# Output weights of six head pairs in 2, 4 or 8 loads of fewer partitions instead of one load of 128

## The chip, the cores and the metric

The kernel runs on one core of a Trainium2 chip. The metric is the device time of one execution in microseconds (us). A core has a matrix engine (TensorE, PE in the profile; its weight loads are PEld), VectorE (DVE), ScalarE (ACT), GpSimd (POOL), and SyncE (SP), which here does nothing but wait on semaphores and issue transfers. Transfers are carried out by 16 DMA engines. On-chip memory (SBUF) has 128 partitions; a tile's first dimension is its partitions.

## The reference

One token goes through a gated mix of two blocks: `out = g*a + (1-g)*b`, with `g = sigmoid(sum(x * gate_w))`. Block b is a layernorm of `x` (448 numbers), a small MLP over 1792 hidden units with a tanh-gelu, and a sum; it needs little data. Block a is attention for one query token with 16 query heads and 8 key/value heads over a cache of 65536 positions of 256 numbers, bf16:

```python
q = (x @ wq)                                  # 448 -> 16 heads x 256
k = jnp.repeat(k_cache, 2, axis=1)            # k_cache, v_cache: [1, 8, 65536, 256]
v = jnp.repeat(v_cache, 2, axis=1)
scores = jnp.einsum("bhqd,bhkd->bhqk", q, k) * (Dh ** -0.5)
p = softmax(scores, axis=-1)
o = jnp.einsum("bhqk,bhkd->bhqd", p, v)
a = o.transpose(0, 2, 1, 3).reshape(B, Sq, Hq * Dh) @ wo   # wo: [4096, 448]
```

Both caches are read once: 2 x 8 x 65536 x 256 x 2 bytes, 536.9 MB. The output weights `wo` are 3.67 MB, or 448 KB for the two query heads that share one key/value head (a pair).

## The kernel before

The work is cut into `NP` = 32 blocks, four (`PPH`) for each of the `H` = 8 pairs. A block is 16384 positions: 8 MB of keys and 8 MB of values, laid out as 64 KB in each of the 128 partitions. For a block j, TensorE transposes the keys (L355), VectorE and ScalarE copy the transposes out of the accumulation memory (L675, L820), and TensorE forms the scores (L376). The maximum over the block follows (L681 to L692, L393, L395), then the exponentials (L807) and, one block later, the products with the values (L400 for the denominators, L407). After the fourth block of a pair, TensorE brings the pair's result into the form that the output projection takes (L457) and multiplies it with `wo_sb` (L468), adding up over the pairs in `prj`.

All large loads are issued by SP, in one program order, on one DMA queue. Keys go into a ring of one and a half blocks (`kring`), so a key load can be issued once the first half of the block before has been transposed: SP waits on `sem_tr` (L290). Values have a single buffer (`vbuf`), so the value load of block j waits until the products of block j-1 are done: SP waits on `sem_pv` (L276). In the steady part of the loop the order is: key load j (L300), value load j-1 (L277), key load j+1, value load j, and so on. The loop over j is written out when the program is built, so it is straight-line code on SP.

The output weights have one buffer, `wo_sb`, of 128 partitions x 3584 bytes (`wo_rows` is the same memory as a flat row for each partition). Pair 0's weights are loaded at the start. For pairs g = 1 to 6, `load_v` issues the whole 448 KB (L259) right after the value load of the pair's first block, block 4g, and before that it waits on `s_proj` (L280), that is until the projection of pair g-1 has read the buffer. Partition p gets rows 4p to 4p+3 of the pair's 512 rows of `wo`, which lie one after another in memory, 3584 bytes. TensorE waits for the weights on `sem_wo` (L567), just ahead of the projection. The weights of pair 7 come in two loads of their own near the end (L316, `sem_wl`); the change doesn't touch these.

SP's loop, in short:

```python
for j in range(NP):
    ...                        # wait for kring space; key load j
    if j < LEAD:               # LEAD = 2
        load_v(j)              # waits for vbuf, value load, and at j = 4g the weights
    elif j > LEAD:
        load_v(j - 1)
```

Of the kernel before, what the change touches and what calls it, by code (L numbers as in the profile page):

```python
# [12 lines left out]
def bass_gated_mix__gqa_block_cached__mixer_token_mlp__decode_kernel(  # L13
# [17 lines left out]
    H = A_k_cache.shape[1]  # L31
    T = A_k_cache.shape[2]
    DH = A_k_cache.shape[3]
    DM = A_x.shape[-1]
    HQ = A_wq.shape[1] // DH
    REP = HQ // H
    F = B_w1.shape[1]
    FT = F // 128
    P = 128
# [13 lines left out]
    PPH = NCPH // BODY  # L53
# [42 lines left out]
    with ctx:  # L96
# [6 lines left out]
        def new_sem(name):  # L103
            return ctx.enter_context(nc.semaphore(name))
# [17 lines left out]
        wo_rows = wo_sb[:, :, :].rearrange("p h n -> p (h n)")  # L122
# [82 lines left out]
        sem_wo = new_sem("sem_wo")  # L205
# [34 lines left out]
        s_proj = new_sem("s_proj")  # L240
# [9 lines left out]
        def src(cache, j, n0=0, n1=NV):  # L250
            g, m = divmod(j, PPH)
            s = cache[0, g, m * BODY * CH:(m + 1) * BODY * CH, :].rearrange("(p n) d -> p n d", p=P)
            return s[:, n0:n1, :].rearrange("p n d -> p (n d)")

        @block.sync
        def _(eng):
            def load_wo(g):
                w = A_wo[g * REP * DH:(g + 1) * REP * DH, :]
                eng.dma_start(wo_rows, w.rearrange("(p i) n -> p (i n)", i=2 * REP)).then_inc(sem_wo, 16)  # L259

            load_wo(0)
            eng.dma_start(wq_s.rearrange("p u n -> p (u n)"),
                          A_wq.rearrange("r n -> (r n)").rearrange("(p m) -> p m", p=P)).then_inc(sem_wq, 16)
            def load(dst, cache, j, n0, n1, at, sem):
                eng.dma_start(dst[:, at + n0:at + n1, :].rearrange("p n d -> p (n d)"), src(cache, j, n0, n1)
                              ).then_inc(sem, 16)

            load(kring, A_k_cache, 0, HV, NV, 0, sem_k)
            load(kring, A_k_cache, 0, 0, HV, 0, sem_kb)

            def load_v(j):
                if j == 0:
                    eng.wait_ge(s_q, 1)
                    eng.wait_ge(s_hb, 1)
                else:
                    eng.wait_ge(sem_pv, j)  # L276
                load(vbuf, A_v_cache, j, 0, NV, 0, sem_v)  # L277
                g, m = divmod(j, PPH)
                if m == 0 and 1 <= g < H - 1:
                    eng.wait_ge(s_proj, g)  # L280
                    load_wo(g)

            for j in range(NP):
                if j == LEAD + 1:
                    eng.wait_ge(sem_tr[NB - 1], BODY * LEAD)
                    load(kring, A_k_cache, j, HV, NV, HV, sem_kc[1])
                    eng.wait_ge(sem_tr[NB - 1], BODY * LEAD + DC // 2)
                    load(kring, A_k_cache, j, 0, HV // 2, HV, sem_kq[0])
                if j >= 1:
                    eng.wait_ge(sem_tr[NB - 1], BODY * (j - 1) + DC)  # L290
                if j == LEAD:
                    load(kring, A_k_cache, j, HV, NV, 0, sem_k)
                    load(kring, A_k_cache, j, 0, HV, 0, sem_kc[0])
                elif j == LEAD + 1:
                    load(kring, A_k_cache, j, HV // 2, HV, HV, sem_kq[1])
                elif j == NP - 1:
                    load(kring, A_k_cache, j, 0, HV, HV, sem_k)
                    load(kring, A_k_cache, j, HV, NV, HV, sem_kc[2])
                elif j >= 1:
                    load(kring, A_k_cache, j, 0, NV, HV * (j % 2), sem_k)  # L300
                if j < LEAD:
                    load_v(j)
                elif j > LEAD:
                    load_v(j - 1)


            for (n0, n1), sem in zip(pieces, sem_vp):
                if n0 == 0:
                    eng.wait_ge(sem_tr[NB - 1], BODY * (NP - 1) + DC)
                elif n0 == NRING:  # L310
                    eng.wait_ge(sem_pv, NP - 1)
                load(kring if n1 <= NRING else vbuf, A_v_cache, NP - 1, n0, n1, 0, sem)
            eng.wait_ge(s_proj, H - 1)
            for h in range(REP):
                w = A_wo[(HQ - REP + h) * DH:(HQ - REP + h + 1) * DH, :]
                eng.dma_start(wo_sb[:, h, :], w.rearrange("(p j) n -> p (j n)", j=2)).then_inc(sem_wl[h], 16)  # L316
            eng.wait_ge(s_fin, NCG)
            eng.dma_start(out_ap, out_row[:, :]).then_inc(sem_out, 16)
            eng.wait_ge(sem_out, 16)
# [16 lines left out]
        def _(pe):  # L336
# [45 lines left out]
            def keys(c0, j, *where):  # L382
                j1 = pe.snap(j + 1, min_val=1, max_val=NP)
                transposes(0, c0, j, *where)
                for k in range(1, BODY):
                    transposes(k, c0 + k, j, *where)
                    scores(k - 1, c0 + k - 1, j1)
                scores(BODY - 1, c0 + BODY - 1, j1)


            def maxima(j1):
                pe.wait_ge(s_mcol, j1)
                pe.transpose(mxT, mcol[:, :], ident[:, :]).then_inc(s_mT, 1)  # L393
                pe.wait_ge(s_mdiag, j1)
                pe.matmul(mxB, mones[:, :], mdiag[:, :], start=True, stop=True).then_inc(s_mB, 1)  # L395
# [36 lines left out]
            def piece_wait(n):  # L432
                for (n0, _), sem in zip(pieces, sem_vp):
                    if n == n0:
                        pe.wait_ge(sem, 16)
# [25 lines left out]
            def clear(bank):  # L461
                pe.matmul(bank, ones_sq[0:1, :], zrow[0:1, 0:bank.shape[-1]], start=True, stop=True,
                          skip_group_check=True)
# [67 lines left out]
            with nc.Fori(0, NP + 1, 1, engines=on, head_slot={pe.engine: 0}) as jj:  # L531
                j = pe.snap(jj, min_val=0, max_val=NP)
                m = pe.snap(m_reg, min_val=0, max_val=PPH)
                with pe.If(m >= PPH):
                    pe.reg_add(g_reg, g_reg, 1)
                g = pe.snap(g_reg, min_val=1, max_val=H + 1)
                with pe.If(j > LEAD):
                    maxima(pe.snap(j, min_val=1, max_val=NP))
                with pe.If(j < NP):
                    c0 = pe.snap(j * BODY, min_val=0, max_val=NC)  # L540
                    u16 = pe.snap(j * 16 + 16, min_val=16, max_val=16 * NP)
                    keys(c0, j, u16, pe.snap(x2_reg, min_val=0, max_val=NV))
                with pe.Else():
                    pe.wait_ge(s_mix, 1)
                    for q in range(NCG):
                        r = slice(32 * q, 32 * q + 1)
                        pe.matmul(prj[r, 0:WG], rest[r, :], brow[r, :], start=False, stop=True,
                                  skip_group_check=True)
                with pe.If(j > MIX0):
                    with pe.If(j < MIX0 + FT + 1):  # L550
                        pe.wait_ge(s_pb, pe.snap(mix_reg, min_val=1, max_val=FT))
                        pe.reg_add(mix_reg, mix_reg, 1)
                        for q in range(NCG):
                            pe.matmul(prj[32 * q:32 * q + 1, WG:2 * WG], w2cur[:, :],
                                      gu[:, q * WG:(q + 1) * WG], start=False, stop=True, skip_group_check=True)
                with pe.If(j < LEAD):
                    maxima(pe.snap(j + 1, min_val=1, max_val=NP))
                with pe.If(j != LEAD):
                    values(j, pe.snap(v_reg, min_val=1, max_val=NP))
                    pe.reg_add(v_reg, v_reg, 1)  # L560
                with pe.If(m >= PPH):
                    with pe.If(j < NP):
                        g1 = pe.snap(g - 1, min_val=1, max_val=H)
                        pe.wait_ge(s_cp, g1)
                        clear(acc[:, 0:NACC])
                        by_row(acc[:, SELC:NACC]).then_inc(s_sel, 1)
                        pe.wait_ge(sem_wo, pe.snap(g * 16 - 16, min_val=16, max_val=16 * H))  # L567
                        pe.wait_ge(s_oTn, g1)
                        project(range(2 * REP)).then_inc(s_proj, 1)
                        pe.reg_mov(m_reg, 0)  # L570
                pe.reg_add(m_reg, m_reg, 1)
                pe.reg_sub(x2_reg, NV, x2_reg)
# [286 lines left out]
```

## Time and profile before

| | |
|---|---|
| median of two runs | 1264.39 us (1264.08 and 1264.7) |
| span of the profiled execution, first to last instruction | 1262.9 us (its own time outside the span is not given; the median is 1.49 us above this span) |
| PE busy | 964.6 us, 76% |
| ACT busy | 544.5 us, 43% |
| DVE busy | 500.2 us, 40% |
| data read from HBM | 544.22 MB, 431 GB/s over the span |
| SP's DMA queue (q1), share of 16 DMA engines | 99.7% |

How to read it: the profile was taken in one execution. The page gives the busy time of each engine, then the span in 40 equal slices with one digit for each, the tenths of the slice in which the engine was busy. The DMA row is the mean busy share of the 16 DMA engines, the GB/s row what they moved. A chain of waits follows the work that ended last back to the start. "L355" is a line of the kernel. A wait is given as the engine and line that waited, what released it, the total in us, how many times, and the longest.

### The profile page before, as it was taken

To read this page: it belongs to the slowest core of one execution; us is meant where nothing else is said; L and a number is where in the kernel's file an instruction comes from. 1 tells how busy PE (TensorE), PEld (TensorE's weight loads), DVE (VectorE), ACT (ScalarE), POOL (GpSimd) and SP (SyncE) were. 2 spreads that over 40 slices of the span, in tenths; PEclk is the share of its full clock that TensorE was granted. 3 is DMA by queue.
4 is the path that set the end of the run, shared out by engine and by line. 5 is a ranking of instruction groups with operands and counts; after the bars stand their busy time and mean duration, and the time that the engine had idled before them with its cause. 6 is when DMAs were issued, how large, how long until landed. Compare 5 with 4: busy or idle time off the path is not lost.

```text
span 1262.9 us, 39617 instructions
## 1 busy us (share of the span) xinstructions
PE 964.6 (76%) x17024; PEld 881.7 (70%) x17024; DVE 500.2 (40%) x1128; ACT 544.5 (43%) x692; POOL 0.9 (0%) x7
## 2 busy tenths in 40 slices
PE   4768877688777797767878678876679867698786
PEld 3667876678766687666777667776678756687674
DVE  4334434444544435444444433343333423334342
ACT  2444543345533445333554334443344533345451
POOL 0000000000000000000000000000000000000000
PEclk8779887888878888888987879888798878888897
DMA  9999999999999999999999999999999999999998
GB/s 417 431 421 426 449 432 432 430 432 444 432 434 430 434 432 432 432 434 436 436 434 428 439 432 432 432 440 432 434 432 434 428 440 436 434 432 434 423 438 365
DMA packets 12053, 544.35 MB, mean 431 GB/s; under 512 B 1417, under 2 KB 1676, under 8 KB 2828
## 3 DMA queue, kind: packets, MB, share of 16 engines
q1 hardware_dynamic: 11954, 544.22, 99.7%
q8 instruction: 6, 0.10, 0.0%
q10 hardware_dynamic: 90, 0.01, 0.0%
q14 instruction: 3, 0.02, 0.0%
HBM read 544.22 MB, written 0.00 MB: 431 GB/s over the span
## 4 chain that ended last, share of the span: by engine, by line
DMA 60%; PE 36%; issue 2%; DVE 2%; DVEq 0%; ACT 0%; SPq 0%
DMA kring<-in_A_k_cache_dram 57%; PE kst L355 26%; PE sps L376 6%; DMA vbuf<-in_A_v_cache_dram 3%; PE acc L407 3%; PE acc L457 0%; PE prj L468 0%; PE sps L395 0%; DVE ktT L675 0%; DVE accs L709 0%; PE acc L400 0%; ACT z_b L825 0%; PE sps L393 0%; DVE mrow L686 0%; DVE z_b L656 0%
## 5 line engine op out<-in xcount | busy, mean ns | idle before, releaser
L355 PE MATMUL kst<-ident,kring 128*128 128x128 f32 x4096 | 556.9, 296 | 189.5 <-DMA kring<-in_A_k_cache_dram 166.6
L820 ACT ACTIVATE ktT<-kst 128x1024 bf16<-128x1024 bf16 x512 | 498.6, 1021 | 338.7 <-PE kst L355 338.3
L355 PEld LDWEIGHTS kst<-ident,kring 128*128 128x128 f32 x4096 | 505.1, 154 | 198.6 <-issue 192.3
L675 DVE COPY ktT<-kst 128x1024 bf16<-128x1024 bf16 x512 | 353.9, 692 | 436.0 <-PE kst L355 410.4
L376 PEld LDWEIGHTS sps<-qcur,ktT 128*128 128x128 bf16 x8192 | 238.0, 97 | 2.6
L376 PE MATMUL sps<-qcur,ktT 128*128 128x2 bf16 x8192 | 236.6, 163 | 0.0
L407 PE MATMUL acc<-vbuf,pT 128*2 128x256 bf16 x4008 | 160.0, 335 | 6.5 <-DMA vbuf<-in_A_v_cache_dram 3.7
L407 PEld LDWEIGHTS acc<-vbuf,pT 128*2 128x2 bf16 x4008 | 110.8, 102 | 47.6 <-issue 4.4
L803 ACT ACTIVATE fade<-mdif 128x2 f32<-128x2 f32 x32 | 6.5, 203 | 302.1 <-DVE mdif L692 302.1
L686 DVE TENSOR_REDUCE mrow<-sps 2x1 f32<-2x128 f32 x32 | 8.9, 278 | 159.9 <-PE sps L393 159.9
L395 PEld LDWEIGHTS sps<-mdiag,mones 2*128 2x128 f32 x64 | 11.2, 217 | 28.0 <-DVE mdiag L688 28.0
L807 ACT ACTIVATE pT<-sps,mneg 128x64 f32 x128 | 30.4, 335 | 0.0
L395 PE MATMUL sps<-mdiag,mones 2*128 2x2 f32 x64 | 13.9, 285 | 21.3 <-DVE mdiag L688 21.3
L393 PE MATMUL sps<-ident,mcol 128*2 128x128 f32 x32 | 9.0, 282 | 27.3 <-issue 25.8
L825 ACT ACTIVATE z_b<-z_b 128x448 bf16<-128x448 bf16 x14 | 8.1, 576 | 48.1 <-DVE z_b L662 48.1
L400 PE MATMUL acc<-pT,ones_sq 128*128 128x32 bf16 x256 | 12.0, 182 | 21.9 <-issue 18.4
L709 DVE COPY accs<-acc 128x288 f32<-128x288 f32 x8 | 3.7, 458 | 62.4 <-PE acc L407 62.4
L393 PEld LDWEIGHTS sps<-ident,mcol 128*2 128x2 f32 x32 | 2.6, 80 | 36.2 <-issue 28.1
L681 DVE TENSOR_REDUCE mcol<-sps 128x2 f32<-128x256 f32 x32 | 13.5, 423 | 33.8 <-PE sps L376 33.8
L400 PEld LDWEIGHTS acc<-pT,ones_sq 128*128 128x128 bf16 x256 | 8.8, 99 | 26.0 <-issue 22.3
L704 DVE TENSOR_SCALAR acc<-acc,fader 128x256 f32<-128x256 f32 x32 | 15.8, 493 | 2.5
L497 PE MATMUL kst<-vbuf,xcol 128*64 128x512 bf16 x28 | 5.5, 571 | 8.8 <-DMA vbuf<-in_A_wq_dram 8.8
(111 smaller groups left out, 173.9 us busy)
## 6 DMA issues: line engine op xcount, KB each, us to landing
kring<-in_A_k_cache_dram SPq DMA_DIRECT2D x7, 4096.0 KB, 26.4
kring<-in_A_v_cache_dram SPq DMA_DIRECT2D x1, 4608.0 KB, 27.6
kring<-in_A_k_cache_dram SPq DMA_DIRECT2D x2, 2048.0 KB, 15.1
vbuf<-in_A_wq_dram SPq DMA_DIRECT2D x1, 3584.0 KB, 12.0
wo_sb<-in_A_wo_dram SPq DMA_DIRECT2D x7, 448.0 KB, 25.5
vbuf<-in_A_v_cache_dram SPq DMA_DIRECT2D x1, 1536.0 KB, 9.3
vbuf<-in_A_v_cache_dram SPq DMA_DIRECT2D x1, 1024.0 KB, 11.4
vbuf<-in_A_v_cache_dram SPq DMA_DIRECT2D x1, 768.0 KB, 12.8
```

The source lines that it names most:

```text
L355: ins = pe.transpose(kst[:, b, i * P:(i + 1) * P], kring_f[:, at + NT * (k % DC) + 4 * b + i, :], ident[:, :])
L376: ins = pe.matmul(sps[:, 0, 2 * (NT * k + nt):2 * (NT * k + nt) + 2], ktT[:, par, b, ntl * DH + dj:(ntl + 1) * DH:2], qcur[:, dj, :], star ...
L393: pe.transpose(mxT, mcol[:, :], ident[:, :]).then_inc(s_mT, 1)
L395: pe.matmul(mxB, mones[:, :], mdiag[:, :], start=True, stop=True).then_inc(s_mB, 1)
L400: pe.matmul(acc[:, DENC:SELC], ones_sq[:, :], pT[:, r, :], start=False, stop=(r == BODY - 1), skip_group_check=True)
L407: ins = pe.matmul(acc[o:o + REP, 0:DH], pT[:, r, 2 * nt:2 * nt + 2], buf[:, n, :], start=False, stop=False, skip_group_check=True)
L675: vec.tensor_copy(ktT[:, k % KTB, b, :], kst_b[:, b, :]).then_inc(sem_ev[b], 1)
L681: vec.tensor_reduce(out=mcol[:, :], in_=scores_all.rearrange("p (n hh) -> p hh n", hh=REP), axis=AX.X, op=ALU.max)
L686: vec.tensor_reduce(out=mrow[:, :], in_=mxT, axis=AX.X, op=ALU.max)
L704: vec.tensor_scalar(acc[:, 0:DENC], acc[:, 0:DENC], fader[:, :], None, op0=ALU.mult).then_inc(s_acc, 1)
L807: ins = act.activation(pT[:, bass.ds(p0, DC), hh:2 * NT:REP], scores_all.rearrange("p (a r n hh) -> p a hh r n", a=2, r=DC, hh=REP)[:, hal ...
L820: act.activation(ktT[:, k % KTB, b, :], kst_b[:, b, :], AF.Copy).then_inc(sem_ev[b], 1)
```

## The change

Each load of pairs 1 to 6 is cut into parts of fewer partitions. A table gives for each pair the number of parts and whether a part takes partitions next to each other (0) or every 2nd, 4th or 8th partition (1, "spread"): pair 1 has 4 spread parts of 32 partitions, pair 2 has 4 of 32 next to each other, pair 3 has 2 spread of 64, pair 4 has 8 spread of 16, pair 5 has 2 of 64 next to each other, pair 6 has 8 of 16 next to each other. A partition's 3584 bytes stay in one piece.

The parts no longer go out together. Part i is issued in slot i: slot 0 is the old place, behind the value load of block 4g, with the same wait on `s_proj` ahead of it; slot 1 is behind the key load of block 4g+2, slot 2 behind the value load of block 4g+1, slot 3 behind the key load of block 4g+3, and so on to slot 6, behind the value load of block 4g+3. In the two pairs with eight parts, parts 6 and 7 both go into slot 6. Loads issued for the six pairs go from 6 to 28. The counts on `sem_wo` are scaled so that each pair adds 128 in all, and TensorE's wait is scaled with them.

```diff
-                eng.dma_start(wo_rows, w.rearrange("(p i) n -> p (i n)", i=2 * REP)).then_inc(sem_wo, 16)
+                eng.dma_start(wo_rows, w.rearrange("(p i) n -> p (i n)", i=2 * REP)).then_inc(sem_wo, 128)
+
+            SPLIT = {1: (4, 1), 2: (4, 0), 3: (2, 1), 4: (8, 1), 5: (2, 0), 6: (8, 0)}
+
+            def load_wo_parts(g, slot):
+                if not 1 <= g < H - 1:
+                    return
+                if slot == 0:
+                    eng.wait_ge(s_proj, g)
+                w = A_wo[g * REP * DH:(g + 1) * REP * DH, :].rearrange("(p i) n -> p (i n)", i=2 * REP)
+                parts, spread = SPLIT[g]
+                n = P // parts
+                for i in range(parts):
+                    if min(i, 6) == slot:
+                        rows = slice(i, P, parts) if spread else slice(i * n, (i + 1) * n)
+                        eng.dma_start(wo_rows[rows, :], w[rows, :]).then_inc(sem_wo, 128 // parts)
...
                 load(vbuf, A_v_cache, j, 0, NV, 0, sem_v)
-                g, m = divmod(j, PPH)
-                if m == 0 and 1 <= g < H - 1:
-                    eng.wait_ge(s_proj, g)
-                    load_wo(g)
+                load_wo_parts(j // PPH, 2 * (j % PPH))
...
                     load(kring, A_k_cache, j, 0, NV, HV * (j % 2), sem_k)
+                if j % PPH != 1:
+                    load_wo_parts((j - 2) // PPH, 2 * ((j - 2) % PPH) + 1)
                 if j < LEAD:
                     load_v(j)
...
-                        pe.wait_ge(sem_wo, pe.snap(g * 16 - 16, min_val=16, max_val=16 * H))
+                        pe.wait_ge(sem_wo, pe.snap(g * 128 - 128, min_val=128, max_val=128 * H))
```

## The prediction

> **What bounds the kernel now.** I read the page's slices and its queue table first, to see whether any resource is full all the way.
>
> ```profile
> span 1262.9 us, 39617 instructions
> ...
> DMA  9999999999999999999999999999999999999998
> GB/s 417 431 421 426 449 432 432 430 432 444 432 434 430 434 432 432 432 434 436 436 434 428 439 432 432 432 440 432 434 432 434 428 440 436 434 432 434 423 438 365
> DMA packets 12053, 544.35 MB, mean 431 GB/s; under 512 B 1417, under 2 KB 1676, under 8 KB 2828
> ...
> q1 hardware_dynamic: 11954, 544.22, 99.7%
> ```
>
> The 16 DMA engines are at 90% or more in 39 of 40 slices, and the queue that SP feeds takes 99.7% of them. No slice has a hole; the dip in the last is the computing after the last load. Next I asked who waits: on the page's groups the matrix engine stands idle ahead of the key transposes, and the chain of waits is mostly key loads.
>
> ```profile
> DMA 60%; PE 36%; issue 2%; DVE 2%; DVEq 0%; ACT 0%; SPq 0%
> ...
> L355 PE MATMUL kst<-ident,kring 128*128 128x128 f32 x4096 | 556.9, 296 | 189.5 <-DMA kring<-in_A_k_cache_dram 166.6
> ```
>
> PE lost 166.6 us to key loads, so it has slack in nearly every block, and the 36% of PE in the chain must not be read as a bound: those are stretches in which the next load was already waiting in a busy queue. The chain in order of time, from the second pair's first blocks to the third's, shows this. Each row is a key load: start at its issue, then the us until it has landed.
>
> ```profile
> 219.94 27.82 DMA kring<-in_A_k_cache_dram
> ...
> 259.47 27.01 DMA kring<-in_A_k_cache_dram
> ...
> 297.61 27.57 DMA kring<-in_A_k_cache_dram
> ...
> 335.77 28.11 DMA kring<-in_A_k_cache_dram
> ...
> 375.55 28.09 DMA kring<-in_A_k_cache_dram
> ...
> 414.26 28.09 DMA kring<-in_A_k_cache_dram
> ```
>
> The landings are at 247.76, 286.48, 325.18, 363.88, 403.64 and 442.35. Their distances are 38.72, 38.70, 38.70, 39.76 and 38.71 us. The issues, by contrast, are 38.1 to 39.8 us apart, so the landings keep a beat that the issues don't: it is set by the queue. In 38.70 us one key block and one value block land, 2 x 8 MB = 16.777 MB, 433.5 GB/s. The one longer distance holds, besides, the weights of pair 2.
>
> So the end moves by what the change adds to the queue's work, and by nothing else unless the queue runs dry.
>
> **What the weights cost now.** 39.76 - 38.70 = 1.06 us for the 448 KB. At 433.5 GB/s, 458,752 bytes take 1.058 us. The load thus costs its bytes, and its price as one more transfer in a full queue is 0.00 us, give or take 0.02 for the rounding of the four ends. Six such loads are 6.4 us, and as the bytes stay the same, the 6.4 us stay.
>
> **22 more transfers.** 28 instead of 6. What a transfer adds besides its data shows in a window of the DMA view, 195 to 250 us, in which four transfers land (key, value, weights, key):
>
> ```profile
> DMA packets 550, 23.92 MB, mean 435 GB/s; under 512 B 64, under 2 KB 64, under 8 KB 192
> ...
> wo_sb<-in_A_wo_dram SPq DMA_DIRECT2D x1, 448.0 KB, 24.8
> ```
>
> 64 packets under 512 B for four transfers are 16 for each, one on each DMA engine, and the 128 others under 8 KB are the weights' 128 rows. The change keeps the 128 rows of a pair whole, so it adds 22 x 16 = 352 short packets and nothing else. By the 0.00 to 0.02 us above, 22 transfers cost 0.0 to 0.4 us; I take 0.3, near the upper end, since a part has fewer rows between its short packets than any load of this queue.
>
> [...]
>
> **Fewer partitions for each transfer.** This is the unknown. Every large load of the trace covers 128 partitions, so no row tells how 16, 32 or 64 share the 16 DMA engines. Bounds from the 1.06 us row: at best a part costs its bytes, 1.06/n for n parts, and the sum over a pair is unchanged: 0. At worst a part costs what a whole load costs, 1.06 us, as it would if each DMA engine served a fixed eighth of a 128-row load, all others stood still meanwhile: 28 x 1.06 - 6 x 1.06 = 23.3 us. Below nothing it can't go: the engines are full already, and the bytes are the same. I take 1.0 us. The row that it is nearest to is the 448 KB load that costs its bytes, and a DMA engine with no row in a part has the next load, already queued, to go on with; since the parts of a pair cover all 128 partitions once, an engine left out of one part has more to do in another, and the queue as a whole loses little.
>
> **Does the queue run dry?** It would if SP issued later than the queue empties. SP's own timeline around the first weights in question, with the window's landing above:
>
> ```profile
> 162.67 0.33 SPq L265 DMA_DIRECT2D vbuf<-in_A_v_cache_dram  x1
> 180.99 0.33 SPq L265 DMA_DIRECT2D kring<-in_A_k_cache_dram  x1
> 199.90 0.33 SPq L265 DMA_DIRECT2D vbuf<-in_A_v_cache_dram  x1
> 203.62 0.33 SPq L259 DMA_DIRECT2D wo_sb<-in_A_wo_dram  x1
> 219.94 0.33 SPq L265 DMA_DIRECT2D kring<-in_A_k_cache_dram  x1
> 237.69 0.33 SPq L265 DMA_DIRECT2D vbuf<-in_A_v_cache_dram  x1
> ...
> 1245.33 1.75 SPq L265 DMA_DIRECT2D vbuf<-in_A_v_cache_dram  x4
> 1247.12 0.91 SPq L316 DMA_DIRECT2D wo_sb<-in_A_wo_dram  x2
> ```
>
> The weights issued at 203.62 landed 24.8 us later, at 228.42, so the key load issued at 219.94 had 8.5 us of queued work ahead. The value load issued at 237.69 had the key load ahead until 247.76, 10.1 us. These two covers are what hides every delay on SP. A part takes SP 0.33 us to issue; at most two follow each other, 0.66 us, and behind each of them SP waits 16 us or more for `sem_tr` or `sem_pv` (199.90 to 219.94, 219.94 to 237.69), so the issue costs nothing. Slot 0 gets less data than before, at least 1.06/8 instead of 1.06, so the next key load finds 0.9 us less ahead: 7.6 us, still cover. Were it gone, each us of lateness would be a us of empty queue. Nor does more in flight hold SP up: near the end it issues six loads in 2.7 us without a pause.
>
> The wait on `s_proj` stays where it was, with the same one key load behind it.
>
> ```profile
> SPq L259 <- PE prj L468: 18.8, 6, 3.4
> ```
>
> Its 3.4 us at most lie inside the same 16 us of waiting.
>
> **Does the projection get its weights late?** Here the change is real: a part in slot 6 is queued behind the pair's last value load, where the weights used to land three blocks earlier. TensorE's queue stands still at the wait on `sem_wo`, the next block's maxima and transposes behind it. The same point of pair 0, for times:
>
> ```profile
> 169.43 6.35 PE L355 MATMUL kst<-ident,kring 128*128 128x128 f32 x32 [4.62 <-DMA kring<-in_A_k_cache_dram]
> ...
> 194.53 5.33 PE L407 MATMUL acc<-vbuf,pT 128*2 128x256 bf16 x128
> ...
> 202.68 0.91 PE L468 MATMUL prj<-wo_sb,oTn 128*1 128x224 bf16 x8 [0.41 <-DVE oTn L733]
> ...
> vbuf<-in_A_v_cache_dram SPq DMA_DIRECT2D x31, 28.1
> ```
>
> The last value load was issued at 162.67 and, at the median of 28.1 us, landed at 190.8. Two parts of 56 KB behind it add 0.3 us by their bytes, 2.1 us at the worst price above: 191.1 to 192.9. The weights are read at 202.68. Cover 9.8 us or more, cost 0.
>
> **Sum.** 0 (bytes) + 0.3 (22 transfers) + 1.0 (fewer partitions) + 0 (issue, waits) = 1.3 us. The profiled span becomes 1262.9 + 1.3 = 1264.2; the median of the runs is 1.49 us above the span, and on it the forecast is 1265.7 us.
>
> **Rivals.** First, parts of few partitions slow the queue. For it: a transfer to 16 partitions may make several DMA engines write into the same part of the on-chip memory, and all of them are at their limit. Against it: they queue other work, as said. [...] Chance 0.27.
>
> Second, the one that ends slower: each further transfer on the queue carries a fixed price that a single 448 KB load between two large ones hid, because its short packets waited behind other data. It sits at the end of every part, 22 times. It passes 2% (25.3 us) at 1.15 us for each. The load of pair 2 says 0.00, which speaks against it; with the price at the 3.4 us in which the quickest weight load landed as a whole, less 1.06, it is 22 x 2.3 = 51 us, 1316.
>
> ```profile
> DMA to landing us min/median/max: 3.4/25.5/26.3
> ```
>
> [...]
>
> Third, faster: smaller bites ahead of the key loads let PE start earlier. PE does get key blocks 4g+2 up to 0.9 us earlier, but only to wait for later ones. All 544.22 MB at 433.5 GB/s take 1255.4 us, so no more than 7.5 us of the span are there to be won, at the start and the end, which the change leaves alone. Chance 0.03, nearly all of it for a drop of a us or so below the runs shown; 0.01 is left for 2%.
>
> **Numbers.** The forecast case has 0.66 and its own range is 1263.3 (the runs' spread, no price at all, and a few tenths besides) to 1267.5. The range reaches on into the first rival, to 1275, where its likelier half ends; out are its upper end (some 0.10), the second rival and most of the third. Two per cent is about what a measurement of this kernel can tell from no change. Faster by more: 0.01. Slower by more: 0.04 of the second rival and 0.01 for the far end of the first, 0.05. Within: 0.94.
>
> **What would show it.** In the profile of the changed kernel: 352 more packets under 512 B (1769) with the DMA row still at 9; key landings 38.70 us apart where no part lies between, and longer by 1.06/n for each part where one does, 1.06 over each pair; adjacent and spread pairs alike; no wait of PE's projection on the weights; SP's wait on `s_proj` near 18.8 us. [...] A digit below 9 in the DMA row inside the loop would mean that the queue ran dry, which I hold to be excluded by covers of 7.6 us and more.

## The result and the profile after

The changed kernel takes 1277.4 us (median of 1276.16 and 1278.64) against 1264.39 before: 1.0102 times, with a 95% interval of 1.0073 to 1.0131. That is 13.0 us more where 1.3 were forecast, and above the stated range, whose top was 1275. The profiled execution took 1276.16 us with a span of 1274.9, 12.0 us longer than the span before. The run times here and below are medians; one execution, 1301.06 us in the run with partitions 0 to 63, had a granted clock of 0.746 where the four others had 0.848 to 0.85, and is not counted.

The page of the changed kernel, the same rows as before:

```profile
span 1274.9 us, 39639 instructions
...
DMA  9999999999999999999999999999999999999998
GB/s 421 426 421 428 445 430 440 435 431 434 432 430 414 414 434 428 433 436 434 434 430 430 434 425 431 419 414 416 430 432 438 427 427 417 421 427 430 434 434 364
DMA packets 12405, 544.35 MB, mean 427 GB/s; under 512 B 1769, under 2 KB 2028, under 8 KB 3180
...
q1 hardware_dynamic: 12306, 544.22, 99.8%
```

The DMA engines are as busy as before, the bytes are the same, and there are exactly the 352 further short packets that were expected (1769). What has dropped is the GB/s row: 414 in slices 13 and 14, 414 to 419 in slices 26 to 28, 417 and 421 in slices 34 and 35. The engines are busy and move less. So the queue didn't run dry; the packets themselves got longer.

Where they did, the chain of waits tells by the key loads, as before: start at the issue, then the us until landing.

```profile
298.14 27.03 DMA kring<-in_A_k_cache_dram
...
375.49 28.67 DMA kring<-in_A_k_cache_dram
...
415.16 30.05 DMA kring<-in_A_k_cache_dram
...
456.17 28.09 DMA kring<-in_A_k_cache_dram
...
536.79 25.43 DMA kring<-in_A_k_cache_dram
...
572.73 28.71 DMA kring<-in_A_k_cache_dram
...
807.95 28.82 DMA kring<-in_A_k_cache_dram
...
848.21 30.64 DMA kring<-in_A_k_cache_dram
...
889.74 28.78 DMA kring<-in_A_k_cache_dram
...
930.04 27.18 DMA kring<-in_A_k_cache_dram
```

Landings, worked out as issue plus duration: 325.17, 404.16, 445.21, 484.26, 562.22, 601.44, then 836.77, 878.85, 918.52 and 957.22. From 325.17 to 404.16 lie two blocks and the first quarter of pair 2: 2 x 38.70 + 0.265 = 77.67 us by the bytes, and 78.99 were taken, 1.32 more. The next two distances are 1.82 and 0.09 over. Pair 3 lies in 484.26 to 562.22 and on to 601.44: 77.96 and 39.22, which are the bytes to 0.03 us. Pair 5, the same two parts of 64 partitions but next to each other, lies in 42.08 and 39.67: 2.85 and 0.44 over. The block after it, without a part, is back at 38.70. A distance can hold the price of the part that follows the key load too, since that load's last rows are still moving when the part begins; the sum over a pair doesn't depend on that.

Over all pairs:

| pair | parts | partitions of a part | us beyond the bytes |
|---|---|---|---|
| 1 | 4 | every 4th | 0.0 |
| 2 | 4 | 32 adjacent | 3.2 |
| 3 | 2 | every 2nd | 0.0 |
| 4 | 8 | every 8th | 2.0 |
| 5 | 2 | 64 adjacent | 3.3 |
| 6 | 8 | 16 adjacent | 3.4 |

The sum is 11.9 of the 12.0 us between the spans. What each pair's stretch moved shows in the windows view, here 40 us from the first part of pair 3 and 40 us from that of pair 5; the last two columns are the DMA share and the GB/s:

```profile
539.00:579.00 40.00, 33.23 (x611) 30.89 (x610) 19.33 (x42) 20.40 (x26) 0.00 (x0) 0.87 1.00 434
...
852.00:892.00 40.00, 27.72 (x496) 25.52 (x493) 12.32 (x26) 15.39 (x20) 0.00 (x0) 0.83 1.00 400
```

The share is 1.00 in both; 434 GB/s against 400. The trace's packet records (start, duration and size of each packet, but not its engine or its partition) say which packets are long. While a part of pair 3 moves, the 64 KB rows of keys and values around it take 2.42 us each, as everywhere, and the part's own 3584-byte rows 140 ns. While a part of pair 5 moves, its own rows take 140 to 305 ns, and 24 of the 30 neighbouring 64 KB rows take longer than 2.45 us, up to 4.04. Summed over the whole run and shared over 16 engines, the 64 KB rows took 10.9 us longer than before, the 3584-byte rows of the weights 0.9. So some nine tenths of the loss sits in loads that the change didn't touch.

### The profile page after: what moved, and what is told of

It reads as the page before. It is cut to its first block, busy times and chain, and to the rows that moved or that the text cites. A ratio compares the mean times of both kernels' runs of the same rounds, so it can differ in the third digit from the quotient of the medians.

```text
span 1274.9 us, 39639 instructions
## 1 busy us (share of the span) xinstructions
PE 969.6 (76%) x17024; PEld 885.4 (69%) x17024; DVE 500.0 (39%) x1128; ACT 545.1 (43%) x692; POOL 0.9 (0%) x7
## 2 busy tenths in 40 slices
DMA packets 12405, 544.35 MB, mean 427 GB/s; under 512 B 1769, under 2 KB 2028, under 8 KB 3180
## 4 chain that ended last, share of the span: by engine, by line
DMA 63%; PE 34%; issue 1%; DVE 1%; DVEq 0%; ACT 0%; SPq 0%
DMA kring<-in_A_k_cache_dram 60%; PE kst L369 25%; PE sps L390 6%; DMA vbuf<-in_A_v_cache_dram 3%; PE acc L421 2%; PE acc L471 0%; PE prj L482 0%; PE sps L409 0%; PE acc L414 0%; DVE accs L723 0%; DVE ktT L689 0%; PE sps L407 0%; ACT z_b L839 0%; DVE mrow L700 0%; DVE mdiag L702 0%
## 5 line engine op out<-in xcount | busy, mean ns | idle before, releaser
L421 PE MATMUL acc<-vbuf,pT 128*2 128x256 bf16 x4008 | 163.1, 339 | 7.0 <-DMA vbuf<-in_A_v_cache_dram 3.7
L414 PE MATMUL acc<-pT,ones_sq 128*128 128x32 bf16 x256 | 12.0, 182 | 21.9 <-issue 18.4
## 6 DMA issues: line engine op xcount, KB each, us to landing
vbuf<-in_A_wq_dram SPq DMA_DIRECT2D x1, 3584.0 KB, 11.9
```

Source lines behind the costliest of these rows:

```text
L414: pe.matmul(acc[:, DENC:SELC], ones_sq[:, :], pT[:, r, :], start=False, stop=(r == BODY - 1), skip_group_check=True)
L421: ins = pe.matmul(acc[o:o + REP, 0:DH], pT[:, r, 2 * nt:2 * nt + 2], buf[:, n, :], start=False, stop=False, skip_group_check=True)
```

## The experiments

After the result the question was what makes a part dear. In the table, spread parts of 32 and 64 partitions are free and adjacent ones aren't, but in the change the adjacent partitions also read adjacent stretches of HBM, and each pair differed in several things at once. So the runs give all six pairs the same treatment. Every run is compared with the kernel before on the same chip, which took 1264.08, 1264.25 and 1264.26 us (medians) in the three sets of four runs.

**Adjacent against spread, nothing else.** First all pairs as pair 5, then all as pair 3.

```diff
-            SPLIT = {1: (4, 1), 2: (4, 0), 3: (2, 1), 4: (8, 1), 5: (2, 0), 6: (8, 0)}
+            SPLIT = {g: (2, 0) for g in range(1, 7)}
```

> All six pairs in two parts of 64 partitions next to each other, as pair 5 has them in the changed kernel. There, the key landings around pair 5's parts lay 3.29 us further apart than 38.70 us and the bytes explain (42.08 + 39.67 against 2 x 38.70 + 1.06). If adjacency is the cause, whichever side it acts on, this makes 6 x 3.29 = 19.7 us: 1284 us. If it was something particular to pair 5's place in the run, or the number of parts, the time comes out near 1265 to 1268.

Measured: 1289.69 us, 1.0195 [1.0172, 1.0219], from 1285.7 to 1292.28. That is 25.6 us, 2.1 for each of the 12 parts, more than the 1.64 of pair 5 alone.

```diff
-            SPLIT = {1: (4, 1), 2: (4, 0), 3: (2, 1), 4: (8, 1), 5: (2, 0), 6: (8, 0)}
+            SPLIT = {g: (2, 1) for g in range(1, 7)}
```

> All six pairs in two parts of every second partition, as pair 3 has them, whose key landings showed 0.03 us beyond the bytes. With adjacency as the cause, on either side: 1264.4 to 1265 us, no change from the kernel before, although the loads, slots and short packets are those of the run with adjacent parts. If the splitting itself costs, it is several us above 1264.4.

Measured: 1264.23 us, 1.0001 [0.9992, 1.0011]. The number of loads, the slots, the waits and the packets are those of the run before; only the choice of partitions differs, and with it which rows of `wo` a part reads. Key loads around pair 3, in the chain of the adjacent run and then of the spread run:

```profile
463.27 27.90 DMA kring<-in_A_k_cache_dram
543.74 29.73 DMA kring<-in_A_k_cache_dram
```

```profile
454.12 26.73 DMA kring<-in_A_k_cache_dram
531.11 27.68 DMA kring<-in_A_k_cache_dram
```

From landing to landing, 82.30 us against 77.94. The bytes of two blocks and half of the pair's weights ask for 77.93. So neither the six further transfers nor slots 0 and 1 cost anything here.

**Which side: HBM or SBUF?** In these two runs the source rows and the target partitions are chosen apart; in both, all pairs have two parts.

```diff
-                        rows = slice(i, P, parts) if spread else slice(i * n, (i + 1) * n)
-                        eng.dma_start(wo_rows[rows, :], w[rows, :]).then_inc(sem_wo, 128 // parts)
+                        near, far = slice(i * n, (i + 1) * n), slice(i, P, parts)
+                        eng.dma_start(wo_rows[far, :], w[near, :]).then_inc(sem_wo, 128 // parts)
```

> As the run with spread partitions, but each part reads 64 weight rows that lie next to each other in HBM (so a pair's weights go to other partitions than they should: the projection of pairs 1 to 6 is computed with rows in the wrong order). Write-side theory (the collision is at the partitions written): 1264.4 to 1265. Read-side theory (16 DMA engines reading a stretch of half the length): 1284.

Measured: 1264.28 us, 1.0004 [0.9994, 1.0014].

```diff
-                        eng.dma_start(wo_rows[far, :], w[near, :]).then_inc(sem_wo, 128 // parts)
+                        eng.dma_start(wo_rows[near, :], w[far, :]).then_inc(sem_wo, 128 // parts)
```

> The reverse: adjacent partitions, filled from every second group of weight rows in HBM (again in the wrong order for the projection of pairs 1 to 6). Write-side theory: 1284. Read-side theory: 1264.4 to 1265. A value half way, near 1274, would say that both sides take part.

Measured: 1286.17 us, 1.016 [1.0126, 1.0195]. That is 22.1 us, about what adjacent parts cost when they also read adjacent rows (25.6, from 21.6 to 28.2 in single executions). So the price follows the partitions written; the read-side theory falls.

**Closeness, carrier or coverage?** Three things could be wrong with 64 adjacent partitions: that they are close, that the DMA engine that writes a partition here isn't the one that writes its keys and values, or how they are laid over the 128 (in one half or in both, densely or thinly), which this text calls coverage. One load per pair, half the bytes:

```diff
-            SPLIT = {1: (4, 1), 2: (4, 0), 3: (2, 1), 4: (8, 1), 5: (2, 0), 6: (8, 0)}
+            SPLIT = {g: (1, 0) for g in range(1, 7)}
...
-                        rows = slice(i, P, parts) if spread else slice(i * n, (i + 1) * n)
-                        eng.dma_start(wo_rows[rows, :], w[rows, :]).then_inc(sem_wo, 128 // parts)
+                        rows = slice(0, 64)
+                        eng.dma_start(wo_rows[rows, :], w[rows, :]).then_inc(sem_wo, 128)
```

> One load per pair, partitions 0 to 63 only, in the old place; the upper half of the weights of pairs 1 to 6 is left out (pair 0's stay there). Bytes: 6 x 0.53 = 3.2 us less than before, 1260.9 us, if a part alone is harmless. With the price of an adjacent part as measured (25.6 us over 12 parts, 2.1 each): 1260.9 + 12.8 = 1273.7 us. This is the yardstick for the next run.

Measured: 1269.72 us, 1.0045 [1.0029, 1.0061], from 1268.06 to 1271.2. Beside the next run this is a price of 8.7 us, 1.4 for each load, where 12.8 were expected from parts that go out apart.

```diff
-                        rows = slice(0, 64)
+                        rows = slice(32, 96)
```

> As the run before, but partitions 32 to 95: just as many, just as close, and as many bytes (the outer quarters are left out). [...] Theory 'carrier': what costs is that an engine writes into partitions whose key and value rows another engine carries, whatever the coverage. Then it costs as much as partitions 0 to 63: some 1273 us.

Measured: 1261.04 us, 0.9974 [0.9964, 0.9984], from 1260.81 to 1261.62: what the bytes left out are worth, and no more. Key loads around the same pair, in the chain of the run with partitions 0 to 63, then with 32 to 95:

```profile
454.45 28.09 DMA kring<-in_A_k_cache_dram
533.37 28.24 DMA kring<-in_A_k_cache_dram
```

```profile
453.11 27.15 DMA kring<-in_A_k_cache_dram
530.20 28.03 DMA kring<-in_A_k_cache_dram
```

Landing to landing: 79.07 us against 77.97, with 77.93 by the bytes. Moving the same 64 adjacent partitions up by 32 removes the price. The packet records agree: with 0 to 63, 23 or 24 of 30 neighbouring 64 KB rows are longer than 2.45 us for every pair, with 32 to 95 none. Closeness is out, and coverage fits both runs: 0 to 63 lie in one half, 32 to 95 in both. The carrier theory as put here forecast some 1273 us for both and falls. But which engine writes which row isn't in the records, so a carrier theory of another form is neither shown nor excluded.

**Bytes or transfers?**

```diff
-                        eng.dma_start(wo_rows[rows, :], w[rows, :]).then_inc(sem_wo, 128)
+                        eng.dma_start(wo_rows[rows, 0:DM * REP], w[rows, 0:DM * REP]).then_inc(sem_wo, 128)
```

(in the kernel with partitions 0 to 63)

> Partitions 0 to 63, with half of each row (1792 of 3584 bytes; three quarters of the weights of pairs 1 to 6 are left out). If the price goes by the bytes that collide: 1264.1 - 6 x 0.79 = 1259.3 without it, plus half of 12.8 = 6.4, 1265.7 us. If it is a fixed price per transfer or per row: 1259.3 + 12.8 = 1272.1.

Measured: 1264.3 us, 1.0 [0.999, 1.001]. The bytes saved are 6 x 0.79 = 4.8 us, so 4.8 us came back as price: 0.8 for each load, against (1269.72 - 1261.04)/6 = 1.4 for the whole rows. The price goes about with the bytes.

**Together instead of apart.** Both adjacent halves of a pair in slot 0.

```diff
-                    if min(i, 6) == slot:
+                    if slot == 0:
```

(with two adjacent parts in all pairs)

> Both adjacent halves of each pair behind the same value load, one right after the other, as near as two loads can come to the single load of before. If the spacing over successive loads matters (each half meets key and value rows alone), the two halves together balance and it is near 1264.1 us. If each part collides by itself with rows that are in flight on other engines, about 12 x 2.1 = 25 us as with one part per slot, 1289, perhaps less where the halves overlap each other: over 1275.

Measured: 1278.73 us, 1.011 [1.009, 1.0129], 14.5 us or 1.2 for each part. Cheaper than apart, dearer than one load of the same bytes, which is free: the second half doesn't make up for the first. The profiled span shows it with the queue as full as ever:

```profile
span 1276.8 us, 39623 instructions
...
q1 hardware_dynamic: 12050, 544.22, 99.7%
```

**Spread, but over one half.** The reverse of the test with partitions 32 to 95: parts that aren't adjacent and yet lie in one half, beside the adjacent parts of the same size and the fully spread ones.

```diff
+            SPLIT = {g: (4, 0) for g in range(1, 7)}
```

> All six pairs in four parts of 32 partitions next to each other. In the changed kernel pair 2 had them, and its key landings showed 3.2 us beyond the bytes (78.99 + 41.05 + 39.05 against 4 x 38.70 + 1.06): 1264.2 + 6 x 3.2 = 1283.4 us. [...]

Measured: 1285.38 us, 1.0172 [1.0155, 1.0189], 21.1 us, 0.9 for each of 24 parts.

```diff
+            SPLIT = {g: (4, 1) for g in range(1, 7)}
...
-                        rows = slice(i, P, parts) if spread else slice(i * n, (i + 1) * n)
+                        o = 64 * (i % 2) + i // 2
+                        rows = slice(o, o + 63, 2)
```

> Four parts of 32 partitions, each every second partition of one half (0, 2 to 62; 64, 66 to 126; and the odd ones). [...] Coverage theory: as dear as the adjacent parts, 1283 us, give or take 3. If closeness of the partitions is what costs: 1264 to 1266.

Measured: 1284.06 us, 1.0161 [1.0136, 1.0186], 19.8 us, 0.8 for each part: as dear as adjacent.

```diff
+            SPLIT = {g: (4, 1) for g in range(1, 7)}
```

> Four parts of every fourth partition over the whole range, as pair 1 has them: full coverage, 18 more transfers than before. Coverage theory: no price but that of the transfers, 0.0 to 0.4 us: 1264.2 to 1264.6 us.

Measured: 1264.25 us, 1.0 [0.999, 1.0009]. Key loads around pair 3, in the chain of the run spread over one half and then of the run spread over all:

```profile
540.29 26.79 DMA kring<-in_A_k_cache_dram
578.59 29.41 DMA kring<-in_A_k_cache_dram
```

```profile
531.37 27.33 DMA kring<-in_A_k_cache_dram
569.64 28.30 DMA kring<-in_A_k_cache_dram
```

40.92 us between the landings against 39.24, with 39.23 by the bytes of two parts.

**Every 8th partition.** Eight parts of 16 in all six pairs.

```diff
+            SPLIT = {g: (8, 1) for g in range(1, 7)}
```

> [...] Pair 4's key landings showed 2.04 us beyond the bytes: 1264.2 + 6 x 2.04 = 1276.4 us. If spread partitions were free whatever their coverage, and pair 4 only paid for its number of parts, four_spread would show half of that too.

Measured: 1281.91 us, 1.0135 [1.0118, 1.0152], 17.7 us or 0.37 for each of 48 parts. The sign is as expected, the size is half as large again: pair 4 alone showed 0.26 for each part, as pair 5 alone showed less than six such pairs. Why a part costs more in a run that holds more of them wasn't tried. Spread parts aren't free as such: 16 partitions at a step of 8 pay. They lie in both halves of the partitions, so lying in one half is not all that makes a part dear. No part of 16 partitions was free in any run; whether another choice of 16 would be stays open.

Across the changed kernel and these runs a part in one half, or of 16 partitions, costs 1.2 to 2.1 us with 224 KB, 0.8 to 0.9 with 112 KB, and 0.26 to 0.42 with 56 KB. No run that loads all the weights is faster than the kernel before; the fully spread ones equal it.

## Why the prediction was wrong

**The bound** was read rightly. The queue sets the end; distances without a part are 38.70 us again, and what was added to the queue's work came out at the end almost us for us (11.9 of 12.0).

**The 22 transfers** (0.3 us taken, 0.0 to 0.4 bounded): 18 more in the run with four spread parts gave 1264.25 against 1264.26, so the price is nothing that can be seen. The second rival, a fixed price per transfer, falls with it.

**Fewer partitions** is the step that failed. Its value of 1.0 us measured 11.9. The bounds of 0 and 23.3 held it; the choice between them was wrong, and so was its reason. "A DMA engine with no row in a part has the next load, already queued, to go on with" supposes that a part of few partitions keeps few engines. There is no such engine. Each of the 28 parts left 16 short packets, as many as there are engines, and by the packet records all 16 carry data too. In the changed kernel 16 rows of the load ahead of a part end and 16 rows of the load behind it start. Taken in order of time, start and end lie at least 144, 281 or 554 ns apart in a part of 16, 32 or 64 partitions: one, two or four rows of 140 ns for every engine. The same holds for adjacent and spread parts. So 16 engines write into whatever partitions the part has; the worst case of the bounds, in which an engine keeps to fixed rows (eight of 128, a sixteenth and not the eighth that I wrote) and others stand still, doesn't occur either. The load of 448 KB, taken as the nearest row, covers all partitions and so could tell nothing of the case. I treated full engines as a resource that shares out work without loss, and looked for idle engines. What the runs showed in its place is a loss inside the busy time: a part in one half of the partitions, or of 16 at a step of 8, costs 0.26 to 2.1 us, nine tenths of it in the changed kernel by longer 64 KB rows around the parts, and the parts of 32 or 64 that lie over both halves added nothing beyond their bytes.

**The first rival**, with a chance of 0.27, pointed the right way: the distances grew beyond the bytes in pairs 2, 4, 5 and 6, by 3.2, 2.0, 3.3 and 3.4 us. Few partitions alone don't do it, though: pairs 1 and 3, with parts of 32 and 64, are at 0.0. What the rival left out besides is that the neighbours pay as well: while a part of those four pairs moves, 24 or 25 of the 29 or 30 rows of 64 KB beside it are longer than 2.45 us.

**The covers** held. The DMA share stayed at 1.00. SP's wait on the projection is 18.4 us in six waits, 18.8 before, and in the changed kernel's row for it the longest is unchanged:

```profile
SPq L274 <- PE prj L482: 18.4, 6, 3.4
```

TensorE's projection waited for weights once, 0.3 us, and the same wait, 0.4 us, stood in the trace before; the late slots cost nothing. Most parts took SP longer to issue than the 0.33 us that I used, but the waits behind them covered that as said.

**The range** left out what then happened because it cut the first rival at 1275 on the ground that its likelier half ends there. No row supported that cut. The prices that 1267.5 and 1275 stand for are shown by no run; the runs showed 0.26 to 2.1 us for each part that pays, and 0.0 for parts of 32 or 64 spread over all 128 partitions. Nor is two per cent what a measurement here can just tell from no change: the kernel before took 1263.76 to 1265.77 us in all 51 executions beside the experiments.

## What to carry to other kernels

When a kernel lives on a full DMA queue, a small load must be judged by the partitions it writes as well as by its bytes: here 64 partitions cost nothing beyond their bytes as 32 to 95 or as every second one, and 1.4 us more as 0 to 63. Where a load must be split, the runs speak for parts of every second or every fourth partition: these cost nothing beyond their bytes here, and adjacent halves and quarters, or every eighth partition, 0.26 to 2.1 us for each part. Cutting along the row, with all partitions in every part, wasn't tried. And a resource at 100% busy can still lose: compare what it moves per us, stretch by stretch, and ask of each queued neighbour whether it got longer.

## What was not expected of the hardware

A part's own rows grew by at most 165 ns each (from 140 to 305 in pair 5), while 24 of 30 neighbouring rows, 2.42 us long elsewhere, grew by up to 1.6 us. The loss is two to four times the time that the part's bytes take, for instance 0.85 us for 112 KB that take 0.265. Why the loss is larger than that time isn't shown by these runs. Nor is it shown which rows are stretched: the records don't name the engine or the partition.

The price varied from run to run where nothing else did: 1285.7 to 1292.28 us with two adjacent parts, 1263.93 to 1264.49 with two spread ones.

SP took 327 to 589 ns to issue a part, median 492, as the view of the weights' tile in the changed kernel shows, beside a median of 328 for the whole loads before. The number of partitions isn't all of it: pair 0's whole load took 462 ns in the changed kernel and 402 before, and its count on `sem_wo` had grown from 16 to 128. The reason wasn't sought.

```profile
L274 SPq DMA_DIRECT2D wo_sb<-in_A_wo_dram x28: 327/492/589, 202.2 to 1107.2; - x28
```
